# New issue tables for a fused attention and gated feed-forward kernel, with h summed in four parts and a different start

## The chip, the cores and the metric

The kernel runs on one core of a Trainium2 chip. The metric is the device time of one execution in microseconds (us), median of several executions. Engines: PE is TensorE, DVE is VectorE, ACT is ScalarE, POOL is GpSimd. The granted clock is the share of full speed at which PE's clock ran, averaged over an execution; every run reports it.

## The reference, cut to what matters

```
h   = mab(I, x)          # 32 inducing rows attend over x: (4, 12416, 128)
a   = mab(x, h)          # every row of x attends over the 32 rows of h
g   = a @ w_gate;  val = a @ w_val          # 128 -> 1536
ffn = (gelu(g) * val) @ w_out               # 1536 -> 128
out = a + sigmoid(a @ w_res) * ffn          # 49664 rows, float32
```

mab is a softmax attention; gelu is the exact one. As a = softmax @ h has rank 32, the kernel multiplies h with the first-layer weights once a batch and gets g and val from 32-row products.

## The kernel before: what the argument touches

A batch has 24 groups of 512 rows and one of 128, together 146 product slots. A slot is: gate products into a bank (one buffer for PE's results), Gelu on ACT, value products into another bank, then u = gelu * value on DVE. Each full group then takes 48 second-layer products (f) on PE, and is ended on DVE or, for rows with a star, through ACT. While one batch is in this loop, h of the next is made beside it. The order of issue is written by hand in tables, one row a group:

```
plan_last = [
    "P3 P1 AP Q2 R6GQ G9P *",
    "7AVG5G Q3R 7P6 P7 R4QG Q13 *",
    ...                                  # cut
```

V, Q and P issue one slot's value with 0, 1 and 2 gate halves, G a gate half alone, a number so many f products, R and A the gate and residual of a group that ends, E one block of exponentials of the next batch, c one accumulation for its h. The first batch has `plan_first`, the second and third share `plan`, the fourth has `plan_last`.

```
def background(nb):
    n = TOK // M
    cuts = [0, 20, 40, 60, 80, nblk]     # the accumulations "c": blocks from cut to cut
...                                      # cut
def accumulate(b, j0, j1, first, last):  # 2 products a block into one bank, then on DVE
    ...                                  # nacc = bank, or nacc += bank
```

The start, before the loop:

```
finish_h(0)
turn_h(0)
half = PRE // 2
exps("b", 0, 0, half, bank_g())
first_layer(0, 0)
exps("b", 0, half, WIDE, bank_v())
...                                      # cut
warm = bank_f()
for i in range(5):
    pe.matmul(warm, wG[:, :P], wG[:, :TOK], start=True, stop=True)
```

The softmax here doesn't subtract the row's maximum and nothing guards it: scores larger than these inputs give would overflow.

## Time and profile before

| | before |
|---|---|
| median of the first 3 runs | 773.51 us (773.41 to 775.77) |
| span of the profiled run, granted clock | 770.0 us, 0.992 |
| DVE, ACT, PE busy | 96%, 98%, 96% |
| DVE idle from 40 to 760 us | 13.9 us |

The busy shares say that three engines are nearly full. They don't say which one sets the pace in a given stretch; for that the windows are read. The lines that carry the reading stand in the prediction below.

### The profile page before, as it was taken

To read this page: it belongs to the slowest core of one execution; us is meant where nothing else is said; L and a number is where in the kernel's file an instruction comes from. 1 tells how busy PE (TensorE), PEld (TensorE's weight loads), DVE (VectorE), ACT (ScalarE), POOL (GpSimd) and SP (SyncE) were. 2 spreads that over 40 slices of the span, in tenths; PEclk is the share of its full clock that TensorE was granted. 3 is DMA by queue.
4 is the path that set the end of the run, shared out by engine and by line. 5 is a ranking of instruction groups with operands and counts; after the bars stand their busy time and mean duration, and the time that the engine had idled before them with its cause. 6 is when DMAs were issued, how large, how long until landed. Compare 5 with 4: busy or idle time off the path is not lost.

```text
span 770.0 us, 23903 instructions
## 1 busy us (share of the span) xinstructions
PE 737.0 (96%) x9585; PEld 432.7 (56%) x9585; DVE 743.0 (96%) x739; ACT 752.9 (98%) x1504; POOL 468.2 (61%) x470
## 2 busy tenths in 40 slices
PE   6799999999999999999999999999999999999997
PEld 4545565565655555565655555566565655554655
DVE  7799999999999999999999999999999999999998
ACT  6799999999999999999999999999999999999997
POOL 0538989521699778824477868843376755442444
PEclk9999999999999999999999999999999999999999
DMA  8326696501144866501045777640105431101101
GB/s 340 126 49 149 129 221 154 148 30 43 49 98 109 203 128 199 155 32 43 30 90 91 155 172 153 166 117 30 43 29 124 80 85 43 40 32 43 43 29 60
DMA packets 118449, 78.16 MB, mean 101 GB/s; under 512 B 96672, under 2 KB 99392, under 8 KB 118336
## 3 DMA queue, kind: packets, MB, share of 16 engines
q1 hardware_dynamic: 118336, 76.62, 39.3%
q8 instruction: 75, 1.23, 0.6%
q14 instruction: 38, 0.31, 0.1%
HBM read 27.87 MB, written 25.43 MB: 69 GB/s over the span
## 4 chain that ended last, share of the span: by engine, by line
PE 41%; ACT 37%; issue 11%; DVE 5%; POOL 3%; DMA 2%; SPq 0%; DVEq 0%; ACTq 0%; POOLq 0%
ACT ge L368 27%; PE f L391 19%; PE g L357 10%; PE v L357 7%; ACT th L405 4%; PE g L399 3%; DVE u L362 2%; ACT at L410 2%; ACT fe L419 2%; PE g L162 1%; DMA ge<-in_x_dram 1%; ACT e L166 1%; DVE lo L124 1%; POOL a L273 1%; DMA xf<-in_x_dram 1%
## 5 line engine op out<-in xcount | busy, mean ns | idle before, releaser
L362 DVE TENSOR_TENSOR u<-ge,v 128x1024 bf16<-128x1024 f32 x584 | 671.1, 1209 | 9.3 <-ACT ge L368 1.8
L368 ACT ACTIVATE ge<-g 128x512 f32<-128x512 f32 x1164 | 607.7, 654 | 2.0 <-PE g L357 1.6
L391 PEld LDWEIGHTS <-u 128*128 128x128 bf16 x4656 | 270.8, 98 | 205.7 <-issue 201.0
L391 PE MATMUL f<-wO,u 128*128 128x128 bf16 x4656 | 371.6, 220 | 3.9 <-DVE th L423 0.5
L357 PE MATMUL g<-rt,hgv 32*128 32x512 f16 x1152 | 334.2, 379 | 9.3 <-ACT ge L368 0.4
L357 PE MATMUL v<-rt,hgv 32*128 32x512 f16 x1152 | 221.7, 385 | 1.6 <-DVE u L362 1.0
L424 POOL TENSOR_TENSOR at<-at,th 128x512 f32<-128x512 f32 (+1 forms) x99 | 123.7, 1249 | 137.5 <-DVE th L423 64.8
L357 PEld LDWEIGHTS <-hgv 32*128 32x128 bf16 x2400 | 74.9, 91 | 89.6 <-issue 25.5
L420 POOL TENSOR_TENSOR th<-th,fe 128x512 f32<-128x512 f32 (+1 forms) x35 | 42.2, 1206 | 105.3 <-ACT fe L419 105.2
L294 POOL TENSOR_TENSOR a<-e,z 128x1024 f16<-128x1024 f32 (+1 forms) x48 | 89.9, 1881 | 4.5 <-DMA hgv<-a 2.5
L124 POOL TENSOR_TENSOR lo<-xf,hi 128x1024 f16<-128x1024 f32 x36 | 76.9, 2136 | 0.2
L399 PE MATMUL g<-hra,rt 128*128 128x128 f16 x768 | 71.4, 219 | 2.1
L410 ACT ACTIVATE at<-g 128x512 f32<-128x512 f32 (+1 forms) x100 | 64.8, 654 | 0.6 <-issue 0.5
L405 ACT ACTIVATE th<-g 128x512 f32<-128x512 f32 (+1 forms) x100 | 64.0, 649 | 0.2 <-PE g L399 0.2
L399 PEld LDWEIGHTS <-rt 128*128 128x128 f16 x768 | 51.0, 98 | 13.0 <-issue 10.3
L423 DVE SCALAR_TENSOR_TENSOR th<-th,f 128x512 f32<-128x512 f32 (+1 forms) x65 | 44.0, 676 | 3.8 <-PE f L391 2.5
L118 POOL CAST hi<-xf 128x1024 f16<-128x1024 f32 x36 | 37.4, 1038 | 10.1 <-DMA xf<-in_x_dram 10.0
L421 POOL TENSOR_TENSOR at<-at,fe 128x512 f32<-128x512 f32 (+1 forms) x35 | 42.2, 1205 | 0.0
L162 PEld LDWEIGHTS <-xt 128*128 128x128 f16 x768 | 23.4, 97 | 7.5 <-issue 3.7
L419 ACT ACTIVATE fe<-f 128x512 f32<-128x512 f32 (+1 forms) x35 | 22.3, 637 | 0.0
L273 POOL TENSOR_TENSOR a<-a 128x256 f32<-128x256 f32 (+8 forms) x48 | 20.0, 417 | 3.8
L166 ACT ACTIVATE e<-g 128x512 f32<-128x512 f32 (+2 forms) x39 | 19.8, 601 | 2.2 <-PE g L162 2.0
(113 smaller groups left out, 261.4 us busy)
## 6 DMA issues: line engine op xcount, KB each, us to landing
out_dram<-at SPq DMA_DIRECT2D x96, 256.0 KB, 2.1
xf<-in_x_dram SPq DMA_DIRECT2D x38, 512.0 KB, 4.4
ge<-in_x_dram SPq DMA_DIRECT2D x10, 512.0 KB, 8.3
rt<-a SPq DMA_TRANSPOSE x48, 3.1
xt<-hi SPq DMA_TRANSPOSE x36, 3.6
ge<-in_moe_w_gate_dram SPq DMA_DIRECT2D x1, 512.0 KB, 9.2
ge<-in_moe_w_val_dram SPq DMA_DIRECT2D x1, 512.0 KB, 9.3
ge<-in_moe_w_out_dram SPq DMA_DIRECT2D x1, 512.0 KB, 4.2
```

The lines of the kernel that those rows point to most:

```text
L124: eng.tensor_tensor(lo[:, :w, :P], xf_t.pop((b, k))[:, :w, :], hi_t[b, k][:, :w, :], AL.subtract)
L294: eng.tensor_tensor(a2[:, :n], ev[:, o:o + n, :].unsqueeze(2).to_broadcast([P, n, Q, M]), z[:, o:o + n].unsqueeze(2).unsqueeze(3).to_broad ...
L357: pe.matmul(*t[n], start=True, stop=True)
L362: ve.tensor_tensor(u[:, :n], ge_t.pop(value)[:, :n], v_t.pop(value)[:, :n], AL.mult)
L368: act.activation(ge_t[i][:, h * TOK:h * TOK + n], gb[:, :n], AC.Gelu, bias=0.0, scale=1.0)
L391: pe.matmul(self.ffn[:, k, :], u_t[self.gi, si][:, o:o + P], wO[:, fc, :], start=first, stop=not self.todo, skip_group_check=True)
L399: pe.matmul(bank[:, k * P:(k + 1) * P], rt_t[self.b, self.k][:, self.j0 + k, :], hra_t[self.b][:, s, :], start=True, stop=True)
L405: act.activation(self.th[:, :self.tw], self.mix(0), AC.Tanh, bias=0.0, scale=0.5)
L410: act.activation(self.at[:, :self.tw], self.mix(1), AC.Copy, bias=0.0, scale=1.0)
L420: po.tensor_tensor(th, th, fe, AL.mult)
L423: ve.scalar_tensor_tensor(th, th, 1.0, f, AL.add, AL.mult)
L424: (ve if self.gi == ngrp - 1 else po).tensor_tensor(at, at, th, AL.add)
```

## The change

The intent: the order tables were searched again by annealing against a model of the engines that now includes PE's clock; h is summed in four accumulations instead of five; at the start one conversion goes to ACT, the first exponentials come in smaller pieces, and two of the five warm-up products go. The diff, with most table rows cut:

```diff
-            convert_hi(0, tiles[n], act if n in (1, 4, 7) else ve)
+            convert_hi(0, tiles[n], act if n in (1, 4, 7, 10) else ve)
...
     exps("b", 0, 0, half, bank_g())
+    exps("b", 0, half, WIDE // 2, bank_g())
     first_layer(0, 0)
-    exps("b", 0, half, WIDE, bank_v())
+    exps("b", 0, WIDE // 2, WIDE, bank_v())
...
-    for i in range(5):
+    for i in range(3):
         pe.matmul(warm, wG[:, :P], wG[:, :TOK], start=True, stop=True)
...
     plan_last = [
-        "P3 P1 AP Q2 R6GQ G9P *",
-        "7AVG5G Q3R 7P6 P7 R4QG Q13 *",
+        "VGGR4G Q QA8G P8 GQ5 1P6G *",
+        "Q4G RQ6 P4 3AQ 3GQ 8P *",
...    (all 75 rows of the three tables differ)
-        cuts = [0, 20, 40, 60, 80, nblk]
+        cuts = [0, 24, 48, 72, nblk]
```

## The prediction

PE ran at half clock (0.50) from 30.24 to 33.65 us and from 593.44 to 600.26 us, for 3.413 and 6.827 us, then again from 767.52 us, and at 1.00 in between. The second and third of these starts lie 165 and 216 times 3.413 us behind the first (in after's trace, with starts at 30.91, 37.73 and 768.18 us, 2 and 216 times). So in what follows a trace is cut into windows of 3.41 us, counted from these starts. The array work of a window is the columns of each matmul that starts in it, times its share of the array's 128 rows and 128 columns (the trace gives both, as 32*128 for a gate product), over 16 products of 512 columns (before's warm-ups, at full clock, start 0.216 us apart, so 15.8 of them would fit). The windows ahead of the first two slow stretches hold 0.22 and 0.34 of full work so counted; the lightest steady one that was followed by full clock, at 361.3 us, 0.375. With these step 1 compares its 0.39; how much work keeps the clock up is not shown by one trace.

Two remarks of the prediction in numbers: of 933 Gelus from 46 to 760 us that still run when the next one starts, 102 are more than 0.52 us ahead of it, where the median is 0.48, so the starts slip there without any idle time being shown (each of these records names a semaphore to wait for); and the five warm-ups take 1.25 us because the last is recorded with 0.38.

> **What bounds the kernel now.** I read the page's first two parts, then busy time by stretches, then the groups of instructions, the waits of VectorE (DVE), and a timeline around each place that stood out. The page first: three engines are all but full, so no single removal can pay more than the little idle time that is left.

> ```profile
> PE 737.0 (96%) x9585; PEld 432.7 (56%) x9585; DVE 743.0 (96%) x739; ACT 752.9 (98%) x1504; POOL 468.2 (61%) x470
> ...
> L362 DVE TENSOR_TENSOR u<-ge,v 128x1024 bf16<-128x1024 f32 x584 | 671.1, 1209 | 9.3 <-ACT ge L368 1.8
> L368 ACT ACTIVATE ge<-g 128x512 f32<-128x512 f32 x1164 | 607.7, 654 | 2.0 <-PE g L357 1.6
> ```

> DVE spends 671 of its 743 us on one product, ScalarE (ACT) 608 of its 753 on one Gelu. Busy intervals of neighbours overlap, so the step from one start to the next is the better measure. One merged run of 19 Gelus lasts 9.53 us: (9.53 - 0.65) / 18 = 0.49 us each. One of 13 products lasts 14.90 us: (14.90 - 1.21) / 12 = 1.14 us each. So 580 full products need 661 us, and 64 full gated sums on DVE, at about 0.60 us of step each, another 38. DVE is as much the bound as ACT, whose higher busy share hides short waits inside overlapping intervals.

> The stretches show where the last per cents lie:

> ```profile
> 20.00:40.00 20.00, 15.94 (x303) 9.62 (x298) 14.84 (x24) 15.65 (x30) 12.02 (x16) 0.91 0.33 107
> 40.00:760.00 720.00, 702.67 (x8960) 408.96 (x8960) 706.14 (x682) 717.67 (x1445) 450.74 (x432) 1.00 0.39 95
> 593.00:600.00 7.00, 7.00 (x50) 3.48 (x48) 5.65 (x5) 5.81 (x13) 5.63 (x7) 0.53 0.34 88
> ```

> The columns are PE, PE weight load, DVE, ACT and POOL busy, then PE's granted clock. In the 720 us of the steady part DVE is idle 13.9 us (720 - 706.1), ACT 2.3 us. About 10 us more of ACT and of DVE idle lies in the first 40 us, before the pipeline runs. And from 593 to 600 us PE ran at half clock: PE is busy without a gap, DVE idles 1.35 us, ACT 1.19. This is the join of the third and the fourth batch.

> The start has its own chain. ACT's timeline there, with what it waited for:

> ```profile
> 33.56 1.28 ACT L541 ACT_TABLE_LOAD   x1
> 34.85 0.20 ACT L541 ACTIVATE gel<-parts 128x1 f32<-128x1 f32 x1
> 35.53 0.60 ACT L368 ACTIVATE ge<-g 128x512 f32<-128x512 f32 x1 [0.48 <-PE g L357]
> ```

> and PE's, ahead of that first Gelu:

> ```profile
> 33.92 1.25 PE L544 MATMUL f<-wG 128*128 128x512 bf16 x5
> 35.11 0.89 PE L357 MATMUL g<-rt,hgv 32*128 32x512 f16 x2
> ```

> The five warm-up products stand directly in front of the first gate products on PE, and ACT waits 0.48 us for those.

> [...]

> **The change part by part.** I compared the instruction streams of both builds. Gelus (1164), products u (584), gate and residual activations (200), evictions of the second layer on ACT (35: 5+7+7+16 before, 4+8+8+15 after) and table loads between exponentials and Gelus (14) are the same in number. So the new tables buy no work off any engine; they can only close waits.

> (1) Warm-ups, 5 to 3. Two 512-column products at about 0.21 us (the five take 1.25[...]) are 0.43 us off PE ahead of the first gates, against ACT's wait of 0.48. Gain: 0.4 us. The risk is in the clock: the window from 33.7 us holds 0.46 of full work, two warm-ups are 0.125 of it, and the earlier gates give back some 0.05. That leaves about 0.39[...].

> (2) First exponentials in pieces. Before, one activation over 28 blocks (896 columns) starts at 30.53 us after 0.81 us of ACT idle. Now blocks 4 to 15 go first, and ACT works on them while PE computes blocks 16 to 31. [...]PE's own sequence, at half clock here, does not shorten. Gain: 0.1 us.

> (3) The tenth conversion moves from DVE to ACT. It takes 0.6 us off a DVE chain (step of a 1024-wide cast) but adds about 0.95 us to ACT, which in that part runs without a gap to 22.3 us and then waits 0.36 and 0.44 us for the last two tiles. Those waits are nearly eaten up. Gain: 0 to 0.1 us.

> (4) h in quarters. The accumulations per batch go from 5 to 4, three times: 3 additions of 0.29 us off DVE, and 3 waits for PE's sum (1.5 us over three of them in the waits, but most others are far shorter; I take 0.1 each). Gain: about 1.0 us. The price: each sum keeps PE for 48 products instead of 40, and a bank for as long.

> (5) Tables. The light place at the third join is four product slots with few second-layer products between them ("P 3P 1AP Q"). Counted in quarters of a 512-column product, these four slots hold 0.27 of what PE could do at full clock in the same DVE time; the lightest four slots at that join afterwards hold 0.36. I give the slow stretch 70% to vanish, worth its 1.2 to 1.35 us: 0.9 us. Of the other 11 us of DVE idle in the steady part (13.9 less 1.35 and the 1.0 of the sums), most lies around the sums and table switches of the next batch; a tenth of it, 1.1 us, is my guess for the anneal. No number in the profile supports more.

> Sum: 0.4 + 0.1 + 0.05 + 1.0 + 0.9 + 1.1 = 3.5 us. From 773.5 us that is **770.0 us**, 0.45%.

> **The rivals.** First, nothing comes of it (773 us): the model in which the tables were annealed is not the chip, [...]the slow stretch appears at another join in another execution, and DVE and ACT have the same work as before. For it: the equal counts; the lightest three-slot runs are equal in both tables (0.30). Against it: the warm-ups and three additions are real. Second, the anneal finds more (766 to 768 us): DVE's 13.9 us of steady idle is all waiting for others, and halving it would give 767. For it: the waits come in clusters, which a better order could spread. Against: the tables were already annealed, and ACT has only 2.3 us of visible idle in the steady part, with semaphore waits between its steps. Third, PE gets colder (774 to 776 us): fewer warm-ups drop the clock at 37 us, or a 48-product sum starves the Gelus; half clock costs about 1.3 us per 6.8 us as seen. Against it: the estimate of 0.39 and the lighter joins' counts.

> **Range and chances.** Before's three runs span 773.4 to 775.8 us, so a plain repeat has 1 us or so of noise. With the rivals at either side I take 766.5 to 773.8 us. Faster by over 2% would be under 758 us, which needs 15 us where DVE's steady idle is 13.9: 1%. Slower by over 2% (789 us) would need many slow windows: 1%.

> **What would show it.** Right if the first Gelu starts near 35.1 us; if the granted clock around 590 to 600 us is 1.00; if DVE's steady idle falls from 13.9 to about 11 us with Gelu and product counts and means unchanged; if the group of nacc additions has 9 members. Wrong if a half-clock stretch stands at another join or right after the start, if DVE's idle moves from the sums to the Gelus, or if ACT's mean per Gelu grows, which would say that the order starves ACT.

## The result, and the profile after

| | before | after |
|---|---|---|
| median, first comparison | 774.16 us (6 runs) | 771.91 us (6 runs) |
| ratio, 95% interval | | 0.9968 (0.9950 to 0.9985) |
| median, repeated with the last experiments | 774.05 us (11 runs) | 772.51 us (6 runs) |
| ratio, 95% interval | | 0.9989 (0.9969 to 1.0009) |
| span of the profiled run, granted clock | 770.0 us, 0.992 | 770.5 us, 0.992 |

A ratio is the mean time of one kernel's runs over that of the other's runs of the same rounds, so it is not quite the ratio of the medians. The first comparison shows a gain of 0.3%; the repeat's interval reaches over 1. Over all runs with a recorded clock, those beside the experiments included, the means are 773.61 us (33 runs of before) and 772.09 us (12 runs of after), a gain of 1.5 us, or 0.2%.

The two profiled runs are equally long, although the medians differ by 2 us. That is the first clue. The page after, its busy shares and the two large groups:

```profile
PE 738.9 (96%) x9583; PEld 432.5 (56%) x9583; DVE 741.2 (96%) x735; ACT 753.3 (98%) x1506; POOL 467.4 (61%) x470
...
L362 DVE TENSOR_TENSOR u<-ge,v 128x1024 bf16<-128x1024 f32 x584 | 671.7, 1212 | 8.2 <-PE g L357 1.9
L368 ACT ACTIVATE ge<-g 128x512 f32<-128x512 f32 x1164 | 608.3, 661 | 2.7 <-PE g L357 1.6
```

The counts of the two large groups are those of before. DVE has four instructions fewer (three additions, and the conversion that went to ACT) and is busy 1.8 us less; ACT has two more and is busy 0.4 us more. So hardly any work went, and nothing of the large groups. The same stretches as before (PE, weight load, DVE, ACT, POOL busy, then the granted clock), and one more, from 36 to 46 us:

```profile
20.00:40.00 20.00, 16.07 (x299) 9.84 (x298) 13.37 (x23) 16.17 (x30) 11.81 (x16) 0.86 0.33 108
36.00:46.00 10.00, 9.61 (x72) 4.35 (x70) 8.37 (x8) 8.86 (x18) 3.23 (x3) 0.66 0.21 41
593.00:600.00 7.00, 6.58 (x65) 3.25 (x63) 7.00 (x9) 7.00 (x18) 5.49 (x6) 1.00 0.49 113
40.00:760.00 720.00, 704.29 (x8962) 408.36 (x8961) 705.62 (x679) 717.70 (x1446) 449.57 (x432) 1.00 0.39 95
```

The half clock at the third join has gone: 1.00 where before had 0.53, and DVE and ACT without a gap. A new one stands right behind the start: PE's clock is at half from 37.7 to 44.6 us. DVE's steady idle did not fall; it is 14.4 us. The chain of the start, ACT first and then PE ahead of the first gates:

```profile
33.76 1.28 ACT L542 ACT_TABLE_LOAD   x1
35.06 0.20 ACT L542 ACTIVATE gel<-parts 128x1 f32<-128x1 f32 x1
35.51 3.77 ACT L368 ACTIVATE ge<-g 128x512 f32<-128x512 f32 x7 [0.25 <-PE g L357]
```

```profile
34.34 0.82 PE L545 MATMUL f<-wG 128*128 128x512 bf16 x3
35.09 0.38 PE L357 MATMUL g<-rt,hgv 32*128 32x512 f16 x1
```

Two warm-ups fewer, and the first gate product starts at 35.09 us instead of 35.11: the three begin 0.4 us later, behind products that ran at half clock (that stretch ended at 34.3 us in this execution, at 33.6 in before's). And DVE has a new wait, for the first sum of h:

```profile
DVE nacc L187 <- PE g L182: 4.2, 2, 2.1
```

Twice 2.1 us, in the second and third batch, where before had no wait at that copy beyond the start.

**Where the time went, product by product.** The start times of single u products on DVE (u20 is the 20th of 584), from the traces, show what a total hides (us from the span's start):

```
                         u1    u20   u146   u292   u438   u470   u584 (last)
before                  36.7  59.6  222.3  406.6  590.4  630.1  765.3
after                   36.9  61.3  223.8  408.5  593.0  630.4  765.4
```

After is 1.7 us later by u20 (the half clock behind the start), 2.6 us later by u438, and then gains 2.3 us between u438 and u470, across the third join. So in these two executions the gain and the losses cancel.

### The profile page after: what moved, and what is told of

The parts are those of the page before. It is cut to its first block, busy times and chain, and to the rows that moved or that the text cites. A ratio compares the mean times of both kernels' runs of the same rounds, so it can differ in the third digit from the quotient of the medians.

```text
span 770.5 us, 23888 instructions
## 1 busy us (share of the span) xinstructions
PE 738.9 (96%) x9583; PEld 432.5 (56%) x9583; DVE 741.2 (96%) x735; ACT 753.3 (98%) x1506; POOL 467.4 (61%) x470
## 4 chain that ended last, share of the span: by engine, by line
PE 47%; ACT 35%; issue 10%; DVE 4%; POOL 3%; DMA 1%; SPq 0%; ACTq 0%; DVEq 0%; POOLq 0%
ACT ge L368 23%; PE f L391 22%; PE g L357 12%; PE v L357 7%; PE g L399 3%; DVE u L362 3%; ACT at L410 3%; ACT th L405 3%; ACT e L166 2%; ACT fe L419 2%; ACT xt L141 1%; POOL lo L124 1%; ACT L166 1%; DMA xf<-in_x_dram 1%; DMA ge<-in_x_dram 1%
## 5 line engine op out<-in xcount | busy, mean ns | idle before, releaser
L362 DVE TENSOR_TENSOR u<-ge,v 128x1024 bf16<-128x1024 f32 x584 | 671.7, 1212 | 8.2 <-PE g L357 1.9
L368 ACT ACTIVATE ge<-g 128x512 f32<-128x512 f32 x1164 | 608.3, 661 | 2.7 <-PE g L357 1.6
L357 PE MATMUL g<-rt,hgv 32*128 32x512 f16 x1152 | 337.7, 380 | 7.3 <-ACT ge L368 0.4
L357 PE MATMUL v<-rt,hgv 32*128 32x512 f16 x1152 | 222.3, 385 | 2.5 <-DVE u L362 1.5
L357 PEld LDWEIGHTS <-hgv 32*128 32x128 bf16 x2400 | 75.3, 91 | 87.8 <-issue 22.8
L166 ACT ACTIVATE e<-g 128x512 f32<-128x512 f32 (+3 forms) x40 | 20.4, 600 | 2.4 <-PE g L162 2.2
```

Of the source, the lines that this page charges most:

```text
L166: act.activation(e[:, (j0 - t0) * M:(j1 - t0) * M], bank[:, :(j1 - j0) * M], AC.Exp, bias=0.0, scale=scale)
L357: pe.matmul(*t[n], start=True, stop=True)
L362: ve.tensor_tensor(u[:, :n], ge_t.pop(value)[:, :n], v_t.pop(value)[:, :n], AL.mult)
L368: act.activation(ge_t[i][:, h * TOK:h * TOK + n], gb[:, :n], AC.Gelu, bias=0.0, scale=1.0)
```

## The experiments

Theory A, formed from this: the tables save no work; their whole gain is that PE's clock falls less often in the steady part. Rival B: the prediction's sum, in which the start is worth 0.5 us, the quarters 1.0 and a better order another 1.1.

### The start alone, and the tables alone

e1_start_only puts the three changes of the start into the kernel before; e2_tables_only is the changed kernel with before's start.

```diff
 # e1, against before            # e2, against after
+ n in (1, 4, 7, 10)            - n in (1, 4, 7, 10)   + n in (1, 4, 7)
+ exps 4..15, then 16..31       - exps in two pieces   + one piece
+ for i in range(3)             - range(3)             + range(5)
```

> The old tables and the old five cuts, with only the three changes of the start (tenth conversion on ACT, first exponentials in two pieces, three warm-up products). Theory A (the start's changes buy nothing: the first Gelu began at 35.51 us after and 35.53 us before, and with two warm-ups less PE fell to half clock from 37.7 us): same as before within 0.5 us, or up to 1.5 us slower, first Gelu at 35.5 us, and a half-clock stretch near 38 us in the profile. Rival B (the prediction's sum: the start is worth 0.5 us): 0.5 us faster than before, first Gelu at 35.1 us.

> The new tables with the four cuts, with the old start (five warm-ups, one piece of exponentials, tenth conversion on DVE). Theory A: all of the gain is here, 2.3 us or more under before, thus as fast as the changed kernel or up to 1 us faster. Rival B: it lacks the start's 0.5 us, so 1.7 us under before and 0.5 us slower than the changed kernel.

e1: 773.77 us, ratio to before 0.9993 (0.9966 to 1.0021), mean clock 0.988. The start's changes are worth nothing that this can see, and its first Gelu began at 35.84 us. The half-clock stretch near 38 us did not come; instead this execution had two in the steady part, told of below. e2: 771.83 us, 0.9971 (0.9944 to 0.9997), mean clock 0.994. So it is as fast as the changed kernel, and the tables with the quarters carry the gain as far as these runs can tell. But the theories lie only 0.5 us apart and the intervals are some 2 us wide to either side, so the times decide nothing between them: e2's 2.0 us under before lies between A's 2.3 and B's 1.7. What speaks against B's sum is e1's first Gelu, which did not come at B's 35.1 us (nor at A's 35.5).

Each run's clock was read as well. The 33 runs of before go from 770.5 us at a clock of 0.995 to 777.2 us at 0.981, correlation -0.95 (-0.92 to -0.96 on each of the three chips used), and the line through them has a slope of 448 us for one unit of clock. A half-clock stretch of t us lowers the mean by t / (2 x 770), so a window of 3.4 us costs 448 x 3.4 / 1540 = 1.0 us. The program is the same in all 33. The 12 runs of the changed kernel lie on average 0.9 us above this line: at equal mean clock the new tables are not the faster ones.

### Five warm-ups again

```diff
 # e3_warm5, against after
-    for i in range(3):
+    for i in range(5):
```

> The changed kernel with five warm-up products again. Theory A (the two warm-ups that went kept the clock up): no half-clock stretch from 37.7 us in the profile, mean granted clock about 0.996 instead of 0.992, and 0 to 1.5 us faster than the changed kernel's 771.9 us. Rival B (warm-ups stand in front of the first gates and cost 0.2 us each): 0.4 us slower than it.

Measured: 770.90 us, ratio to before 0.9963 (0.9937 to 0.9989), mean clock 0.996, and no half clock from 37.7 us. u20 came at 60.4 us instead of 61.3, and that lead was still there at u438 (591.9 against 593.0) and at the last u (764.2 against 765.4). Between these two profiles the half clock behind the start thus makes 0.9 us. Between the kernels as such it isn't settled: the changed kernel's interval (0.9950 to 0.9985) overlaps e3's. It is also not certain protection, as the runs below with five warm-ups and the old tables show a half clock there (37.9 us in one, 39.4 in another); nor do three bring it for certain, as e1 and e6 have three and had full clock there.

### Levelling the light place at the join: two tries

Six products were moved from the end of the third batch to the light slots at the start of the fourth, in the kernel before:

```diff
 # e4_join_level, against before (last row of the third batch, first of the fourth)
-        "P10 P8GG *",
-        "P3 P1 AP Q2 R6GQ G9P *",
+        "P7 P5GG *",
+        "P5 P5 AP Q4 R6GQ G9P *",
```

> The kernel before with six second-layer products moved from the end of the third batch into the light slots at the start of the fourth; nothing else, the same number of instructions. Theory C (the half clock at 593 to 600 us came from too little array work in one window, and cost 1.2 us): clock 1.00 at the join, DVE and ACT idle in 593 to 600 us under 0.5 us each instead of 1.35 and 1.19, and 0.8 to 1.5 us faster than before. Rival D (the half clock there costs nothing as buffers catch up, or it is a matter of phase): same as before within 0.3 us.

Measured: 804.28 us, ratio 1.0399. The edit was wrong: it takes 6 products away and puts 8 in, so the fourth batch ran two products out of step. In the table each group's last f product ends a run of digits, so that gate and value products stand between it and the next group's first. Out of step by two, the next group's f follow at once, into the same single bank, and PE waits for its eviction. The waits of PE, this kernel:

```profile
PE f L391 <- ACT fe L419: 16.6, 17, 1.2
PE f L391 <- DVE th L423: 11.7, 11, 1.6
```

Those are 28.3 us of the 30, where before has 0.5 us for the second. It says nothing on the clock. The same edit with the count kept (18 products of one group as 7, 5, 6, then 12 of the small one as 4, 3, 5):

```diff
 # e10_join_exact, against before
-        "P10 P8GG *",
-        "P3 P1 AP Q2 R6GQ G9P *",
+        "P7 P5GG *",
+        "P6 P4 AP Q3 R5GQ G9P *",
```

> The kernel before with the second-layer products at the join of the third and fourth batch spread evenly (10, 8, 3, 1, 2, 6 between the slots become 7, 5, 6, 4, 3, 5), so that every group still ends at the end of a run of products. Theory A (too little array work in a window halves the clock there, and each us of half clock costs 0.3 us): no half clock at 590 to 600 us, mean clock up by 0.002 to 0.004, and 0.8 to 2 us faster than before. Rival B (clock and time share another cause): within 0.4 us of before. Side theory on the run with two products out of step, which cost 30 us: here nothing of that kind, as no run crosses a group's end.

Measured: 774.14 us, ratio 1.0015 (0.9994 to 1.0037), mean clock 0.986; the half clock at the join was there, 595.4 to 602.2 us. Nothing was won and A's numbers missed: moving work about inside the join does not put more of it there, and the windows ahead of and inside the fall held 0.375 and 0.31 of full array work (counted as said ahead of the prediction). It doesn't decide between the theories, as it failed to move the clock.

### Quarters in the old tables, fifths in the new

```diff
 # e5_quarters_only, against before; one "c" less in plan_first and plan
-        cuts = [0, 20, 40, 60, 80, nblk]
+        cuts = [0, 24, 48, 72, nblk]
 # e6_five_cuts, against after: the opposite, one "c" more
```

> The kernel before with four cuts of h instead of five (one accumulation step taken out of each table), nothing else. Prediction's step 4: 1.0 us faster than before (0.87 us of additions and three short waits less on VectorE). Rival (a step that only lies beside other work is worth nothing, and the longer sums may even hold the bank longer): within 0.4 us of before at equal granted clock.

> The changed kernel with five cuts of h again. If the quarters are worth 1.0 us: 772.9 us. If nothing: 771.9 us as the changed kernel, with the same mean granted clock near 0.995.

e5: median 776.30 us (771.23 to 777.56), ratio 1.0020 (0.9993 to 1.0048), clock 0.987. The three additions went (9 left, 2.6 us of work instead of 12 and 3.5), but the measured time did not fall:

```profile
L190 DVE TENSOR_TENSOR nacc<-g,nacc 128x129 f32<-128x129 f32 x12 | 3.5, 289 | 1.6 <-PE g L182 1.5
L190 DVE TENSOR_TENSOR nacc<-g,nacc 128x129 f32<-128x129 f32 x9 | 2.6, 294 | 2.1 <-PE g L182 2.1
```

That is the group of additions in before and in e5: count, busy us and mean ns, then the idle time ahead of them, 2.1 us where before had 1.6, nearly all of it for PE's products.

e6: 773.94 us, ratio 1.0004 (0.9987 to 1.0021), clock 0.992. With the new tables five cuts cost about as much as all of the gain: from u20 to u438 its profile needs 533.5 us (60.3 to 593.8) against e3's 531.5 with four. e5's profile had half clock in three of its four batches; the first, at full clock, needs 162.4 us from u20 to u146. Before's own profile needs 162.7, but e1, e10 and e12, with the same five cuts and old tables, need 162.2 each (before's execution lost 0.5 us between its 63rd and 77th product). Not even the 0.3 us of one batch's addition shows. So quarters show no gain in a table made for fifths, and fifths cost in a table made for quarters. The new wait of 2.1 us at the first sum is not the quarters' doing: with five cuts it is still 4.0 us in two waits.

### Filling the light slots

To force the clock up without touching an order, an idle product is put ahead of a value product wherever the last three slots hold little array work (20 in before, 18 in after):

```diff
 # e8_before_fill and e9_after_fill, in emit()
             v = v_t[value] = bank_v()
+            if sum(work[1:]) < LIGHT:        # the counting of work is cut
+                pe.matmul(v[:, :TOK], wO[:, 0, :], wG[:, :TOK], start=True, stop=True)
```

> The kernel before, tables untouched, with about 20 idle 512-column products put where the last three product slots hold little array work; each is written to the value bank ahead of the real product that overwrites it. Theory A (all of the gain is the granted clock: in the eleven runs of before the time falls from 777.2 us at a clock of 0.981 to 770.6 at 0.995, and at equal clock the new tables are 1 to 1.5 us slower): clock rises from 0.987 to 0.993 or more, time falls to 769.5 to 771.5 us, at or below the changed kernel, and the spread of 6 us shrinks to under 3. Rival B (the time and the clock share a cause, the clock is only a sign of stalls): the clock rises and the time stays at 773 to 774 us, or worse, by 20 times 0.2 us.

> The same filler rule in the changed kernel (18 products). Theory A: its clock is already 0.995, so there is little to win: 771 to 772 us, within 0.7 us of the changed kernel. Rival B: 0.5 us or more slower, the fillers' own cost on TensorE's queue.

e8: 780.45 us, ratio 1.0079 (1.0060 to 1.0099), clock 0.986. e9: 775.45 us, 1.0025 (1.0006 to 1.0044), clock 0.993. Both are 3 to 7 us slower than without, and the clock did not rise. The fillers stand in PE's queue ahead of the value products that DVE waits for: in e8 DVE idles 19.7 us ahead of its u products, 7.6 of them for gate and 2.4 for value products, where before has 9.3, 1.0 and 0.9 (e8's profile has four falls of the steady clock, before's one, so not all of it is the fillers'). At a slope of 448 us per unit of clock, e8 is 6 us slower than before at the same clock, 0.3 us a filler. As a test of A they failed, because the clock was not moved; what they show is that the light slots were not slots in which PE had time to spare.

### Filling the start's gaps, and the changed kernel again

```diff
 # e11_warm5_startfill (after, five warm-ups) and e12_before_startfill
+    fill(1)                 # 512-column products on data at hand, into a bank nobody reads (def cut)
     finish_h(0)
+    fill(3)
     turn_h(0)
+    fill(1)
```

> The changed kernel with five warm-ups again and five idle 512-column products in the gaps that TensorE has while h of the first batch is finished. Theory A: the half-clock stretch at 28 to 34 us vanishes (mean clock 0.997 or more), and the first Gelu, at 36.4 us in the run with five warm-ups, comes 0.5 to 1.2 us earlier; time 769.5 to 770.5 us, under both kernels. Rival B (the start's chain waits on VectorE and ScalarE, not on TensorE's clock): clock up, time as with five warm-ups alone (770.9 us).

> The kernel before with the same five idle products in the start's gaps, tables untouched. Theory A: the start's half clock vanishes, clock up by about 0.003, 0.5 to 1.2 us faster than before. Rival B: within 0.3 us of before.

> The changed kernel unaltered, beside the three others on the same chip and for a second profile. Theory A: 771.9 us within 0.7, mean clock 0.993 to 0.996, and at most one half-clock stretch outside the start and the end, near 38 us if there is one.

The clock at 28 to 34 us was full in both, so here it did move. e11's first Gelu began at 35.45 us against 36.41 in e3's profile, as A said. But the time did not follow: 771.56 us, ratio to before 0.9979 (0.9960 to 0.9998), against e3's 770.90 us in other rounds. The profile shows where the lead went: a half-clock window at 40.1 to 43.5 us, and by u20 e11 stands at 60.5 us, e3 at 60.4. e12: 775.14 us, ratio 1.0027 (1.0005 to 1.0048), its half clock likewise moved, to 37.9 us for 6.8 us. e12 was thus slower than before, which neither side had forecast (B: within 0.3 us). B was right that clearing the start's half clock brings no time: it is not worth removing this way. e13, the changed kernel again: 772.51 us, as in the table above, at a mean clock of 0.992, just under the 0.993 to 0.996 expected; its profile had half clock from 28.4 to 45.5 us and none until the end, and the half clock it drew at the start put u20 at 62.6 us.

### What all profiles together show

There are thirteen profiles besides the one out of step. With the old tables each profile had half clock in the steady part (after 46 us), with the new ones none. What went with it is the share of full array work in the window before, counted as said ahead of the prediction. In e5, too, the windows ahead of a fall lie whole multiples of 3.413 us apart (41, 68 and 109 times from the first).

```
old tables      fell after a window at (us) with this share of array work
before          590.0 (0.34)
e1              406.3 (0.36)  546.3 (0.38)
e5              223.7 (0.38)  363.6 (0.36)  455.8 (0.33)  595.7 (0.28)
e8              227.9 (0.34)  275.7 (0.34)  555.6 (0.34)  603.4 (0.30)
e10             223.3 (0.36)  592.0 (0.38)
e12             270.0 (0.33)  454.3 (0.39)  594.3 (0.27)
new tables      none in after, e2, e3, e6, e9, e11, e13; lightest steady window 0.38 to 0.39
```

Was it luck that the seven executions of the new tables met no light window? The windows lie differently from execution to execution (a half clock began at 593.4 us in before, at 595.4 in e10), so they can be laid over a trace at every phase (here without those that touch a half-clock stretch). In the six profiles of old tables there is then a full-clock steady window under 0.35 at 59 to 99% of the phases, 1.1 to 2.1 of them on average. In the seven of new tables there is one at 0 to 3% of the phases, and in e6, with its fifths, at 17%. So it was not luck: the new tables hardly leave a light window wherever the windows fall.

And a half clock costs what the slope says. e1 has before's tables: between u292 and u340 it needs 58.4 us with a half-clock window at 409.8 us, before 57.3 without; between u400 and u438 52.0 with one at 549.7, before 50.7 without; between u438 and u470 37.9 without, before 39.7 with two. So 1.1 and 1.3 us for one window, 1.8 for two. In those windows PE is the bound, as these lines of e1 show (PE, weight load, DVE, ACT, POOL, clock), and below them those of before for the same products, at full clock:

```profile
409.80:413.20 3.40, 3.40 (x28) 2.29 (x26) 2.81 (x3) 2.83 (x7) 2.84 (x5) 0.50 0.40 116
549.70:553.10 3.40, 3.40 (x30) 2.29 (x26) 2.44 (x3) 2.60 (x6) 0.00 (x0) 0.50 0.00 0
...
409.60:413.00 3.40, 3.28 (x40) 1.82 (x39) 3.40 (x4) 3.40 (x9) 3.21 (x5) 1.00 0.40 116
548.50:551.90 3.40, 3.40 (x45) 1.93 (x41) 3.40 (x4) 3.40 (x8) 0.00 (x0) 1.00 0.00 0
```

At half clock PE is busy for all 3.40 us and gets through 28 and 30 products instead of 40 and 45, and DVE idles 0.59 and 0.96 us where it had no gap. This also settles whether the clock is only a sign of stalls (rival B of e8 and e10): from u292 to u295 the two executions keep step to 0.01 us, the lag of 1.25 us arises at u296 and u297, inside and right behind the window, and at u305 it is still there. At 549.7 us it is the same, with 1.22 us. The stall does not come before the clock falls, and it is not made good.

Last, what the tables are worth without the clock. For each batch take an execution that had full clock in it, old tables against new (e3), in us of DVE's products:

```
                    u20-146   u146-292   u292-438   u438-584    sum
old, full clock      162.2     184.3      183.8      173.1     703.4   (e1; second and third from before)
new, full clock      162.2     184.7      184.5      172.4     703.8
```

At full clock the new tables are thus 0.4 us slower, not faster (the changed kernel's own profile needs 704.1 us from u20 to the last). All that they gain is the half clock that they avoid.

## Why the prediction was right or wrong

The total was right: 771.91 us lies in 766.5 to 773.8, a gain of 2.25 us (1.5 over all runs) where 3.5 were forecast. Term by term it was mostly wrong, with errors that cancelled: 2.6 of the 3.5 us were forecast for things whose gain did not show, and the clock brought more than its 0.9. That the total fits is luck. Of the prediction's own signs two came true (full clock at 590 to 600 us, 9 additions). The first Gelu started at 35.51 us and not at 35.1, DVE's steady idle did not fall to 11 us, and of the signs of being wrong a half clock right after the start came, and ACT's mean per Gelu grew a little (654 to 661 ns).

- **Step 1, warm-ups, 0.4 us: failed.** The first gates started 0.02 us earlier, as the three left ran behind half-clock products. Where the half clock lay alike (e6 with three, 27.5 to 34.4 us; e3 with five, 27.8 to 34.6 us), three did bring the gates forward by 0.6 us and the first Gelu too, but only 0.2 us of it was left at u20: the wait was rightly read, but the first Gelu hardly moves what follows. The risk named there came true in the changed kernel's profile: the window from 34.3 us held 0.34 of full work (0.39 was estimated), and the clock fell for 6.8 us, which cost 0.9 us against e3.
- **Step 2, pieces, 0.1 us: failed, small.** Twelve products now stand ahead of the first layer, and the table load started at 33.76 us instead of 33.56.
- **Step 3, conversion, 0 to 0.1 us:** nothing visible. DVE's chain got shorter, its wait for the first sum became 1.6 us instead of 0.9, and the sum was read at 26.90 us, where before had 26.89. The start as a whole measured 0.9993, with an interval (0.9966 to 1.0021) that could not show 0.1 us.
- **Step 4, quarters, 1.0 us: failed as stated.** The busy time fell by the 0.9 us that were counted. In the old tables the measured time did not (e5), and in the one batch that its profile has at full clock nothing was gained (162.4 us against 162.2). In the new tables going back to fifths costs 2 us (e6). So the value lies in the fit of table and cuts.
- **Step 5, clock, 0.9 us: right that the half clock would go, size far off.** The half clock at the join vanished, and one such pair costs 1.8 us rather than 1.2 to 1.35: the idle from 593 to 600 us leaves out what DVE loses right behind it. Worse, the profile of before was taken as the typical run. It had a clock of 0.992; the 33 runs average 0.988. From 0.988 to 0.993 (mean of 12 runs) is 0.0054 before rounding, times 448 us: 2.4 us. The measured gain is 0.9 us less; 0.4 us of that is what the new tables lose at full clock, the rest is not explained.
- **Step 5, the rest of the anneal, 1.1 us: failed.** At full clock the new tables are 0.4 us slower; DVE's steady idle rose from 13.9 to 14.4 us, with 4.2 us in a wait that was not there before.

The rivals: the first (the slow stretch appears at another join in another execution) was true of the kernel before, and not of the one after. Its premise that equal lightest three-slot runs mean equal risk did not hold; the counts of four slots, which differed (0.27 and 0.36), told more. The second did not come: DVE's steady idle was not reduced. The third (colder behind the start) was true of both profiles of the changed kernel, though not its 774 to 776 us, as the steady clock gave more back.

What stays open: whether five warm-ups beat three between the kernels as such; why the new tables' first sum waits 2.1 us and what it would bring to mend that; what decides on a window between 0.35 and 0.40, where 7 of 28 were followed by half clock; and a direct test in which an edit raises the steady clock alone. Three kernels tried it (e8, e9, e10), and none moved that clock. That the clock costs the time is shown without such an edit, by executions of the same tables that keep step but for the half-clock windows. That the new tables hold more array work in their lightest windows is read from the traces; that the annealer's clock model is what brought this about is argued, not tested.

## What to carry to other kernels

Read the granted clock of every run beside its time before explaining a few tenths of a per cent: one profile can have fallen on a good or a bad execution, and here 6.7 us of spread in one program went with the clock. Here the only gain that was shown came from a schedule whose lightest steady windows of 3.4 us hold more array work (0.38 to 0.39 of full work, where 0.27 to 0.39 stood ahead of a fall in the old tables), and it could not be had by adding idle products ahead of products that were being waited for. In an order table, keep the counts that other parts rest on: two products out of step cost 30 us.
